# Attention with chunk selection, then a mixture over slots: a third ring buffer, a denser weight plan, and new orders of all steps

## The chip, the core and the metric

The kernel runs on one core of a Trainium2 chip. The metric is device time in microseconds (us) of one launch; lower is better. A core has engines that work side by side, each through its own list of instructions in order: PE (matrix products and transposes; its weight loads are shown as PEld), DVE (vector operations), ACT (activations and copies), POOL (here masks, small copies and the issue of loads) and SP (here the first two loads and the stores). Sixteen DMA engines carry the transfers. The kernel's tiles lie in on-chip memory; results of PE land in PSUM, eight banks of it.

## The reference, cut to what matters

B = 4, H = 8, S = 768, D = 64 for q, k, v; 8 experts with weights of 512 x 1024 and 1024 x 512; 32 slots, 4 for each expert.

```python
def _attn_ref(q, k, v):
    chunk, top_k, nc = 32, 6, S // 32
    k_min, k_max = per-chunk minimum and maximum of k
    ub = sum over d of max(q * k_min, q * k_max)        # bound of a chunk's scores
    ub = where(causal by chunk, ub, -1e9)
    top_chunks = argsort(ub)[..., -top_k:]
    scores = q @ k.T / sqrt(D)
    scores = where(chunk selected and causal, scores, -1e9)
    attn = softmax(scores)
    return attn @ v

def _moe_ref(x, phi, w1, w2):
    logits = x @ phi                                     # (3072, 32)
    d = softmax of logits over all 3072 rows
    slot_input = d.T @ x
    for e in range(8):
        slot_out[e] = relu(slot_input[e] @ w1[e]) @ w2[e]
    c = softmax of logits over the 32 slots
    return c @ slot_out
```

The rows x are the attention's outputs, so the last rows of the attention come before any slot is complete, and every output row needs all experts.

## The kernel before

**Pairs.** A pair is two heads of one batch: 16 pairs, four for each batch. For a pair, q and k are transposed on PE (`transposes`, L232) and evacuated by ACT (`evac_T`, L244). `kmin`, `kmax` and `heads` make the chunk bounds of k on DVE; `qneg` and `qpos` the two signs of q. `ubound` (L289) forms the bounds on PE, `select` (L312) takes the sixth largest on DVE with one small copy on POOL, `ns_transposes` and `evac_ns` turn the unselected chunks into a matrix that `scores` (L339) adds as a penalty. The scores come in six column groups (`GROUPS`; for the last pair `GROUPS_LAST`), each two heads wide in one of two PSUM tiles `p_sc`. `expo` (L363) exponentiates a group on ACT, `mask` (L376) clears the diagonal blocks on POOL, `pv` (L385) multiplies with v, `normalise` (L403) divides, `x_transposes` and `evac_x` give the transposed rows.

**Order.** The instructions of each engine stand in the order in which the program is written. A loop over pairs 1 to 15 reads one string of steps for each kind of pair: PLAIN, LOGITS, SLOTS, AFTER, BEFORE_LAST, FINAL. `sc:2` is the scores of group 2 of this pair, `ex`, `mk` its exponential and mask, `pv:0:1` products for query tiles 0 and 1 of the pair before, `trk`, `trq`, `evk`, `evq`, `kmin`, `kmax`, `bd`, `qsn`, `qsp` belong to the pair two ahead, `ub`, `sel`, `ns`, `evns` to the next pair, `norm`, `xt`, `evx` to the pair two behind. `evqd` is `evq` on DVE. Steps like `moe_logits@2` belong to the batch that ended two pairs ago: logits, maximum, exponentials, dispatch.

**Loads.** POOL issues all loads but the first two, in place in the order: `lv` v of a pair, `lkq` k and q of two pairs into a ring of two buffers (`load`, L160), `lw` as many weight blocks of 1 MB as `wplan` (L574) gives for the pair, `lh:n` a quarter of the last two experts' second weights (`w_half`, 256 KB; in the order of `HALVES`: both experts' upper output columns, then both lower). Weights 0 to 7 are w1; 8 to 13 are w2 of six experts. The first q and k arrive in f32 in the space of weight 13 and are cast (`cast`, L583).

**The end.** After pair 15 the last batch's slot softmax runs (L802 to L841), then the experts: `experts_in` (L870), `relu`, `hidden_T`, `experts_out(f)` for four experts over all 512 output columns, `shared_out(y, f)` and `last_expert_out(y)` for the other four over one half y of the columns. `so_all` holds the slots' outputs. For the first six blocks of 256 rows `out_half` writes the columns of half 1 and later those of half 0; the other six blocks are written whole. SP issues every store.

## Time and profile before

| what | us |
|---|---|
| median of 3 runs | 158.33 (158.31 to 158.43) |
| the profiled execution | 158.78 |
| its span, first to last instruction | 157.1 |
| PE, DVE, ACT, POOL busy | 137.4, 121.6, 121.2, 97.8 |
| bytes read and written | 52.49 MB, 6.29 MB |

Times in the rows below count from the span's start. A timeline row gives the start, the time taken, the engine, line, operation, output and inputs, how many such instructions follow one another, and in brackets how long the engine stood idle before and what ended that. A row of stretches gives the stretch, its length, each engine's busy time with the number of its instructions, the granted clock, the DMA engines' busy share and GB/s as written at the destination. A row of a DMA issue gives the number of transfers, their size and the time from issue to landing. In the slices of the span a digit is tenths of busy time.

### The profile page before, as it was taken

What the parts mean: (1) busy time and instruction counts of PE and PEld (TensorE: products, weight loads), DVE (VectorE), ACT (ScalarE), POOL (GpSimd) and SP (SyncE); (2) the same over time, 40 slices, a digit from 0 to 9 for tenths busy, and PEclk for the clock granted to TensorE, in tenths of its full rate; (3) what the DMA queues carried; (4) which work ended last, traced back from release to release, by engine and by line L of the source; (5) the groups of instructions that cost most, each with busy time, mean ns of one, the idle gap of its engine ahead of it and who ended that gap; (6) DMA issues with size and microseconds to landing.
All of it is one profiled execution on the core that took longest, in us unless ns stands there. A gap on an engine that the chain in (4) does not pass through costs nothing.

```text
span 157.1 us, 6041 instructions
## 1 busy us (share of the span) xinstructions
PE 137.4 (87%) x2485; PEld 91.1 (58%) x2486; DVE 121.6 (77%) x442; ACT 121.2 (77%) x172; POOL 97.8 (62%) x196
## 2 busy tenths in 40 slices
...
DMA  5999999999999999999999999999999999949995
GB/s 152 188 187 211 178 210 213 164 192 215 197 209 196 209 194 211 204 220 172 195 173 211 206 214 177 215 195 214 208 206 212 208 194 197 131 169 384 400 422 230
DMA packets 46171, 33.31 MB, mean 212 GB/s; under 512 B 26304, under 2 KB 41664, under 8 KB 46144
## 3 DMA queue, kind: packets, MB, share of 16 engines
q0 software_dynamic: 41328, 25.86, 113.5%
q1 hardware_dynamic: 4816, 7.08, 12.2%
...
HBM read 52.49 MB, written 6.29 MB: 374 GB/s over the span
## 4 chain that ended last, share of the span: by engine, by line
PE 58%; DVE 22%; ACT 7%; issue 3%; POOL 3%; DMA 2%; DVEq 0%; POOLq 0%; ACTq 0%
PE at_ps L398 11%; PE sc_ps L346 11%; PE sc_ps L356 8%; PE tr_ps L238 6%; ACT e_sb L370 4%; PE xT_ps L420 3%; PE ub_ps L296 3%; DVE mx L317 3%; DVE x_sb L411 3%; ACT o_sb L967 3%; PE h_ps L873 2%; DVE mm L256 2%; DVE mm L262 2%; DMA w_sb<-in_k_dram 2%; PE ns_ps L328 2%
## 5 line engine op out<-in xcount | busy, mean ns | idle before, releaser
L370 ACT ACTIVATE e_sb<-sc_ps 128x768 bf16<-128x768 f32 (+1 forms) x96 | 83.1, 926 | 6.5 <-PE sc_ps L356 5.1
L380 POOL TENSOR_SCALAR_AFFINE_SELECT e_sb<-e_sb 128x256 bf16<-128x256 bf16 x96 | 37.9, 417 | 22.0 <-ACT e_sb L370 21.8
L346 PE MATMUL sc_ps<-qT,kT 64*128 64x384 bf16 (+3 forms) x258 | 37.5, 308 | 2.3 <-ACT e_sb L370 2.0
L356 PE MATMUL sc_ps<-nsT,smask 64*128 64x384 bf16 (+2 forms) x294 | 37.7, 284 | 0.3
L398 PE MATMUL at_ps<-v_t,e_sb 128*128 128x65 bf16 x642 | 27.1, 194 | 0.4 <-DVE x_sb L411 0.2
L398 PEld LDWEIGHTS <-e_sb 128*128 128x128 bf16 x642 | 22.8, 97 | 6.5 <-POOL e_sb L380 2.9
L317 DVE MAX8 mx<-ub_ps 128x8 f32<-128x8 f32 (+1 forms) x192 | 16.9, 164 | 5.8 <-PE ub_ps L306 4.9
L346 PEld LDWEIGHTS <-kT 64*128 64x128 bf16 x258 | 12.6, 93 | 9.5 <-issue 3.5
L356 PEld LDWEIGHTS <-smask 64*128 64x128 bf16 x294 | 14.7, 95 | 3.8 <-issue 1.3
...
L411 DVE TENSOR_TENSOR x_sb<-at_ps,inv 128x768 bf16<-128x768 f32 (+1 forms) x17 | 15.5, 910 | 0.6
L247 ACT COPY kT<-tr_ps 128x768 bf16<-128x768 bf16 x16 | 12.8, 802 | 3.5 <-PE tr_ps L238 3.5
L256 DVE TENSOR_REDUCE mm<-kT 128x24 bf16<-128x768 bf16 x16 | 15.1, 944 | 0.4 <-ACT kT L247 0.4
L262 DVE TENSOR_REDUCE mm<-kT 128x24 bf16<-128x768 bf16 x16 | 15.1, 943 | 0.0
L247 ACT COPY qT<-tr_ps 128x768 bf16<-128x768 bf16 x14 | 11.5, 823 | 3.3 <-PE tr_ps L238 3.3
L145 POOL DMA_DIRECT2D w_sb<-in_moe_w_dram x14 | 10.2, 729 | 0.0
L296 PEld LDWEIGHTS <-qpn 128*128 128x128 bf16 x192 | 6.0, 96 | 6.7 <-issue 3.3
L431 DVE COPY xT_sb<-xT_ps 128x768 bf16<-128x768 bf16 (+1 forms) x15 | 8.0, 536 | 2.2 <-PE xT_ps L420 2.0
L296 PE MATMUL ub_ps<-bd,qpn 128*128 128x48 bf16 x192 | 7.8, 184 | 1.6 <-POOL qpn L276 1.4
L238 PE MATMUL tr_ps<-ident,k_in 128*64 128x128 bf16 x192 | 8.4, 223 | 0.7 <-DVE k_in L585 0.5
L420 PE MATMUL xT_ps<-ident,x_sb 128*128 128x128 bf16 x96 | 8.2, 220 | 0.3 <-DVE x_sb L411 0.3
L238 PE MATMUL tr_ps<-ident,q_in 128*64 128x128 bf16 x192 | 8.4, 223 | 0.0
(155 smaller groups left out, 216.3 us busy)
## 6 DMA issues: line engine op xcount, KB each, us to landing
w_sb<-in_moe_w_dram POOLq DMA_DIRECT2D x14, 1024.0 KB, 12.7
out_dram<-o_sb SPq DMA_DIRECT2D x14, 256.0 KB, 2.5
...
w_half<-in_moe_w_dram POOLq DMA_DIRECT2D x8, 256.0 KB, 11.5
...
```

The source lines that it names most:

```text
L238: nc.tensor.matmul(ps[h * 64:(h + 1) * 64, g, :], lhsT=src[:, h, g * D:(g + 1) * D], rhs=ident, is_transpose=True,)
L247: copy(t.rearrange("d (p g) -> d p g", g=NQT), st.pop((nm + "ps", i)).rearrange("d g p -> d p g"),)
L256: nc.vector.tensor_reduce(mm[:, 0, 0, :], kT, axis=AX.X, op=ALU.min)
L262: nc.vector.tensor_reduce(mm[:, 1, 0, :], kT, axis=AX.X, op=ALU.max)
L296: nc.tensor.matmul(o, lhsT=qpn[:, x, t * P:(t + 1) * P], rhs=bd[:, x], start=(t == 0 and x == 0), stop=False,)
L317: nc.vector.max(mx[:, a, :], ub[:, a, :max(8, 4 * t + 4)])
L346: nc.tensor.matmul(ps[:, h, c:c + w], lhsT=kT[r, kg * P:(kg + 1) * P], rhs=qT[r, qs], start=True, stop=False,)
L356: nc.tensor.matmul(ps[:, h, c + (f - t0) * P:c + (l - t0) * P], lhsT=smask[r, x, kg].rearrange("p a b -> p (a b)"), rhs=nsT[r, (f - x * NJ ...
L370: nc.scalar.activation(e[:, :, :w], st.pop(("scps", i, g))[:, :, :w], func=ACT.Exp, scale=scale)
L380: nc.gpsimd.affine_select(out=e[:, :, c:c + P], in_=e[:, :, c:c + P], compare_op=ALU.is_ge, fill=0.0, base=0, pattern=[[0, 2], [1, P]], ch ...
L398: nc.tensor.matmul(o, lhsT=st["e", i, g][:, h, c:c + P], rhs=v_t[i % NV][:, h, kg, :D + 1], start=(kg == 0), stop=(kg == t),)
L411: nc.vector.tensor_tensor(st["x", b][:, t0:t1, 2 * j:2 * j + 2, :].rearrange("p t h d -> p h t d"), at[:, :, :, :D], inv.broadcast_to([P, ...
```

## The change

- k and q get a third ring buffer, in the space of weight 10. `lkq` loads for pairs i + 7 instead of i + 5. `wplan` gives the same twelve blocks in fewer pairs.
- The first k and q lie in two weights' space and are cast by DVE (one head) and ACT (the other); k's transposes go to two PSUM tiles that ACT and DVE evacuate side by side. `qneg` of pair 0 goes from POOL to DVE. The warm-up products have 512 columns, in new numbers and places. Some first loads are issued earlier.
- Every order string is new. `evqd` is gone. FINAL now holds the last pair's own products, normalisations, transposes and logits in parts (`final`).
- The last pair's groups are cut anew: the sixth holds three off-diagonal blocks, all of query tile 5.
- The slot logits' maximum goes through PE as two bf16 parts instead of f32, and the same for the broadcast; the maximum over the first five tiles of the last batch is taken early (`pma`).
- The three exponentials of `exp_c` become one with windows of 24; `live`, which marks the columns that count, is made from `once` after pair 4.
- `experts_out` works on half of the columns like its neighbours; `so_part` is gone.

```diff
-    [(2, 0, 384, 0)],
-    [(4, 0, 256, 0), (2, 384, 128, 256)],
-    [(3, 0, 384, 0), (1, 512, 128, 384)],
-    [(5, 0, 128, 0), (0, 512, 256, 128)],
+    [(4, 0, 256, 0)],
+    [(2, 0, 384, 0), (0, 512, 128, 384)],
+    [(3, 0, 384, 0), (5, 0, 128, 384)],
+    [(0, 640, 128, 0), (1, 512, 128, 128), (2, 384, 128, 256)],
...
+    for x, nm in enumerate(("k", "q")):
+        spare = w_sb[EARLY - 4][:, x * 4 * NQT * D:(x + 1) * 4 * NQT * D]
+        ring[nm].append(spare.rearrange("p (h c) -> p h c", h=4))
...
-        t = ring[nm][i // 2 % 2][:, 2 * (i % 2):2 * (i % 2 + n)]
+        t = ring[nm][i // 2 % 3][:, 2 * (i % 2):2 * (i % 2 + n)]
...
-    stage = w_sb[EARLY - 1].bitcast(F32).rearrange("p (n h c) -> p n h c", n=2, c=512)[:, :, :, :NQT * D]
-    for n, (nm, src) in enumerate((("k", k), ("q", q))):
-        nc.sync.dma_start(out=stage[:, n], in_=src[0, :2].rearrange("h (p g) d -> p h (g d)", p=P))
+    stage = [w_sb[x].bitcast(F32).rearrange("p (h c) -> p h c", c=512)[:, :2, :NQT * D] for x in range(EARLY - 2, EARLY)]
+    for t, src in zip(stage, (k, q)):
+        nc.sync.dma_start(out=t, in_=src[0, :2].rearrange("h (p g) d -> p h (g d)", p=P))
+    load(1, "k")
...
+    def transposes(i, nm, runs=((0, NQT),), home=(p_tp, "tp")):
+
         src = st.pop((nm, i))
-        for g in range(NQT):
-            for h in range(2):
-                nc.tensor.matmul(
-                    ps[h * 64:(h + 1) * 64, g, :], lhsT=src[:, h, g * D:(g + 1) * D], rhs=ident,
-                    is_transpose=True,
-                )
-        st[nm + "ps", i] = ps
-
-    def evac_T(i, nm, copy=nc.scalar.copy):
+        st[nm + "ps", i] = []
+        for g0, g1 in runs:
+            ps = home[0].tile([P, g1 - g0, P], BF16, name="tr_ps", tag=home[1])
+            for g in range(g0, g1):
+                for h in range(2):
+                    nc.tensor.matmul(
+                        ps[h * 64:(h + 1) * 64, g - g0, :], lhsT=src[:, h, g * D:(g + 1) * D], rhs=ident,
+                        is_transpose=True,
+                    )
+            st[nm + "ps", i].append((g0, g1, ps))
...
+    def evac_T(i, nm, *copies):
 
         t = tp3.tile([P, S], BF16, name=nm + "T", tag=nm + "T")
-        copy(
-            t.rearrange("d (p g) -> d p g", g=NQT),
-            st.pop((nm + "ps", i)).rearrange("d g p -> d p g"),
-        )
+        for (g0, g1, ps), copy in zip(st.pop((nm + "ps", i)), copies or (nc.scalar.copy,)):
+            copy(
+                t.rearrange("d (p g) -> d p g", g=NQT)[:, :, g0:g1],
+                ps.rearrange("d g p -> d p g"),
+            )
...
+    def moe_logits(b, hgs=range(NDG), ps=None, ts=range(NQT)):
         phi = phi_sb
         if ps is None:
             ps = st["lgps", b] = p_tp.tile([P, NQT, NS], F32, name="lg_ps", tag="tp")
         else:
             phi = phi_sb.rearrange("p g (o s) -> p g o s", o=1).broadcast_to([P, NDG, 2, NS])
         xT = st["xT", b]
-        for t in range(NQT):
+        for t in ts:
             for hg in hgs:
                 nc.tensor.matmul(
                     ps[:, t, :], lhsT=xT[:, hg, t * P:(t + 1) * P], rhs=phi[:, hg],
-                    start=(hg == 0 and t == 0), stop=(hg == NDG - 1 and t == NQT - 1),
+                    start=(hg == 0 and t == 0),
+                    stop=(hg == NDG - 1 and t == (NQT - 2 if b == B - 1 else NQT - 1)),
+                    skip_group_check=(b == B - 1 and hg == NDG - 1 and t == NQT - 1),
                 )
+
+    def high(t):
+        return t.bitcast(BF16).rearrange("p (s x) -> p s x", x=2)[:, :, 1]
 
     def moe_copy(b):
         lg = small.tile([P, NQT, NS], F32, name="lg", tag="lg")
...
         nc.vector.tensor_copy(lg, ps)
         st["lg", b] = lg
 
+    def moe_lo(b, eng=nc.vector):
+        eng.tensor_tensor(pm_lo[:, :NS], pm_pad[:, :NS], high(pm_pad)[:, :NS], op=ALU.subtract)
+
     def moe_max(b):
 
         pmT = p_tp.tile([P, P], F32, name="pmT_ps", tag="tp")
-        nc.tensor.matmul(pmT, lhsT=pm_pad, rhs=identf, is_transpose=True)
+        nc.tensor.matmul(pmT, lhsT=high(pm_pad), rhs=ident, start=True, stop=False)
+        nc.tensor.matmul(pmT, lhsT=pm_lo, rhs=ident, start=False, stop=True)
...
+        mb_lo = small.tile([P, 1], BF16, name="mb_lo", tag="mb_lo")
+        nc.vector.tensor_tensor(mb_lo, mb, high(mb), op=ALU.subtract)
+        st["mb", b] = high(mb), mb_lo
...
-        nc.scalar.activation(c_pad[:, :, :, :SPE], c4[:, :, :4], func=ACT.Exp)
-        pairs = c4[:, :, 4:8]
-        pairs = bass.AP(pairs.tensor, pairs.offset, [list(x) for x in pairs.ap[:-1]] + [[1, 2 * SPE]])
-        nc.scalar.activation(c_pad[:, :, :, SPE:3 * SPE], pairs, func=ACT.Exp)
-        nc.scalar.activation(
-            c_pad[:, :, :, 3 * SPE:4 * SPE], c4[:, :, 4:5].broadcast_to([P, NQT, 4, SPE]), func=ACT.Exp)
+        c4 = lc[:, :NQT].rearrange("p t (j s) -> p t j s", s=SPE)[:, :, :4]
+        runs = bass.AP(c4.tensor, c4.offset, [list(x) for x in c4.ap[:-1]] + [[1, WIN]])
+        nc.scalar.activation(c_pad[:, :, :, :WIN], runs, func=ACT.Exp)
...
-    wplan = {2: 1, 3: 1, 4: 1, 5: 1, 6: 1, 9: 1, 10: 1, 11: 1, 12: 2, 13: 2, 14: 1, 15: 1}
+    wplan = {2: 2, 4: 1, 6: 2, 8: 1, 9: 1, 10: 1, 12: 2, 13: 2}
...
+    def cast(n, nm):
+        st[nm, 0] = ring[nm][0][:, :2]
+        nc.vector.tensor_copy(st[nm, 0][:, 0], stage[n][:, 0])
+        nc.scalar.copy(st[nm, 0][:, 1], stage[n][:, 1])
+
+    cast(0, "k")
     warm(8)
-    transposes(0, "k")
-    evac_T(0, "k")
+    transposes(0, "k", ((0, 3), (3, NQT)), (p_sc, "sc"))
+    cast(1, "q")
+    warm(1)
+    evac_T(0, "k", nc.scalar.copy, nc.vector.tensor_copy)
+    transposes(0, "q")
     kmin(0)
     kmax(0)
+    evac_T(0, "q")
+    load(4, "k", 2)
+    load_w(0)
     heads(0)
-    warm(2)
-    transposes(0, "q")
-    evac_T(0, "q")
-    qneg(0, nc.gpsimd)
-    load_w(0)
+    qneg(0)
...
+    warm(10)
     ubound(0)
-    transposes(1, "q")
-    evac_T(1, "q")
     spread_mask(NJ, NQT, nc.scalar.copy)
     select(0)
+    transposes(1, "k", ((0, NQT),), (p_sc, "sc"))
+    evac_T(1, "k")
+    transposes(1, "q", ((0, NQT),), (p_sc, "sc"))
+    evac_T(1, "q")
     load_v(1)
-    warm(5)
+    load(4, "q", 2)
+    warm(3)
     ns_transposes(0)
     evac_ns(0)
     kmin(1)
...
     heads(1)
     qneg(1)
     qpos(1)
+    for g in range(5):
+        scores(0, g)
+        expo(0, g, g < 4)
+        if g == 1:
+            load(6, "k", 2)
+            warm(3)
+        if g == 2:
...
-            if have(i + 5) and i % 2:
-                load(i + 5, "k", 2)
-                load(i + 5, "q", 2)
+            if have(i + 7) and i % 2:
+                load(i + 7, "k", 2)
+                load(i + 7, "q", 2)
...
-    PLAIN = """sc:0 trk sc:1 norm ub ex:0 ex:1 sc:2 lv mk:0 mk:1 evk pv:0 pv:5 sel sc:5 ex:2 xt trq lw pv:1:2:3 ex:5 evq sc:3 kmin sc:4 kmax ex:3 evx ns qsn mk:5 evns ex:4 mk:4 bd mk:2 lkq mk:3 pv:4 qsp"""
-    LOGITS = """sc:0 trk sc:2 ex:0 ex:2 ub norm sc:3 evk lv mk:0 ex:3 pv:0 pv:5 mk:2 pv:1 sc:1 sel xt trq pv:2:3 ex:1 evq sc:5 ex:5 mk:1 kmin sc:4 evx ns moe_logits@2 lw kmax bd evns mk:3 qsn ex:4 mk:5 mk:4 pv:4 lkq moe_copy@2 qsp"""
-    SLOTS = """sc:0 ex:0 moe_max@3 mk:0 sc:1 ex:1 mk:1 ub moe_bound@3 norm sel trk moe_comb@3 evk sc:2 pv:0 pv:1:2 lkq ex:2 sc:3 moe_exp@3 ex:3 mk:3 trq xt pv:3 kmin mk:2 evqd moe_exp2@3 evx kmax bd moe_scale@3 lw sc:4 ex:4 lv mk:4 sc:5 moe_comb2@3 ex:5 mk:5 ns pv:5:4 evns moe_dispatch@3 qsn qsp"""
-    AFTER = """sc:0 trk sc:1 ex:0 ex:1 evk mk:0 ub norm lv sc:2 ex:2 pv:0 sel pv:5 pv:1 sc:5 mk:1 xt pv:2:3 trq ex:5 sc:3 evq ex:3 kmin sc:4 evx ns mk:5 lw kmax pv:4 bdp evns mk:2 mk:3 ex:4 lkq mk:4 qsp moe_ct@4 qsn"""
-    BEFORE_LAST = """sc:0 ex:0 moe_max@3 sc:4 ex:4 mk:4 ub norm moe_bound@3 sel moe_comb@3 trk evk sc:2 mk:0 ex:2 pv:0 pv:1 pv:2:3 sc:1 ex:1 trq evq moe_exp@3 mk:2 mk:1 xt kmin kmax bd sc:3 lv evx lw ex:3 moe_exp2@3 moe_scale@3 pv:4 moe_comb2@3 sc:5 ex:5 mk:3 lkq mk:5 ns evns moe_dispatch@3 pv:5 qsp moe_ct3@3 qsn lh:0 lh:1"""
-    FINAL = """sc:0 ex:0 mk:0 lh:2 sc:1 ex:1 mk:1 lh:3 sc:2 norm ctc ex:2 pv:0:1:2 mk:2 sc:3 ex:3 xt mk:3 evx sc:4 ex:4 mz mk:4 pv:4:5:3 sc:5 ex:5 mk:5"""
+    PLAIN = """sc:0 trk lv sc:1 norm ex:0 ex:1 ub sc:2 pv:0 mk:0 evk pv:5 sel sc:5 mk:1 lw trq xt ex:2 pv:2 ex:5 evq pv:3:1 sc:3 kmin sc:4 kmax ex:3 ex:4 evx qsn ns mk:5 pv:4 mk:4 evns mk:2 mk:3 qsp lkq bd"""
+    LOGITS = """sc:0 trk sc:2 ex:0 ub norm ex:2 sc:3 evk mk:0 lv pv:0 pv:5 pv:1 mk:2 sc:1 sel ex:3 xt kmin pv:2 trq pv:3 ex:1 evq sc:5 lw ex:5 mk:1 sc:4 evx ns kmax bd mk:3 moe_logits@2 evns mk:5 qsn lkq ex:4 moe_copy@2 moe_lo@2 mk:4 qsp pv:4"""
+    SLOTS = """sc:1 ex:1 mk:1 moe_max@3 sc:2 ex:2 mk:2 ub moe_bound@3 norm sel moe_comb@3 trk evk sc:0 sc:3 ex:0 moe_exp@3 lkq ex:3 mk:3 pv:0:1:2:3 trq xt kmin evq moe_exp2@3 evx kmax bd moe_scale@3 lv lw sc:5 ex:5 mk:5 sc:4 ex:4 mk:4 ns evns mk:0 moe_dispatch@3 pv:5 moe_comb2@3 qsn qsp pv:4"""
+    AFTER = """sc:0 lv trk sc:2 ex:0 ex:2 evk ub sc:1 norm pv:0 pv:5 sel ex:1 pv:2 pv:3 mk:0 sc:3 pv:1 mk:2 xt trq lw ex:3 sc:5 kmin evx evq ex:5 sc:4 ns mk:1 kmax bdp pv:4 mk:5 evns ex:4 mk:4 lkq qsp moe_ct@4 mk:3 qsn"""
+    BEFORE_LAST = """lv norm sc:2 ex:2 moe_max@3 sc:4 ex:4 sc:0 moe_bound@3 moe_comb@3 mk:4 lw ub sel sc:3 pv:0 trk evk pv:2 moe_exp@3 pv:3:4:5:1 mk:2 ex:0 trq evq kmin sc:5 ex:3 mk:0 moe_comb2@3 kmax moe_exp2@3 xt ns sc:1 moe_scale@3 mk:3 lkq qsn ex:5 lh:0 evx mk:5 ex:1 qsp lh:1 evns moe_dispatch@3 moe_ct3@3 bd mk:1"""
+    FINAL = """sc:1 sc:0 norm sc:2 ex:1 pv:0 pv:2 pv:3 pv:4 mk:1 ctc pv:5 pv:1 ex:0 ex:2 sc:3 xt mk:0 ex:3 norm1 sc:4 mk:2 ex:4 xt1 mk:3 evx pl:0 evx1 sc:5 mk:4 pl:2 pl:1 nl:0 pl:3 nl:1 xl:0 pl:4 lgt el:0 mz lh:2 ex:5 pl:5 lh:3 xl:1 cs nl:2 lgl:0 xl:2 ela:1 lgl:1 ela:2 pma lgl:2 inv"""
...
+    PARTS = [
+        (0, [(0, 0), (1, 0), (2, 0), (1, 1), (2, 1), (2, 2)], True, True),
+        (1, [(3, 0), (3, 1), (4, 1), (4, 4), (3, 2), (4, 2), (4, 0)], True, False),
+        (2, [(5, 4)], True, False),
+        (1, [(3, 3), (4, 3)], False, True),
+        (2, [(5, 3), (5, 5)], False, False),
+        (2, [(5, 0), (5, 1), (5, 2)], False, True),
+    ]
+    SPANS = [(0, 3), (3, 5), (5, 6)]
...
+        elif name == "pl":
+            pv_part(*PARTS[n])
+        elif name == "nl":
+            normalise(LAST, *SPANS[n], part(n)[0])
+        elif name == "xl":
+            x_transposes(LAST, *SPANS[n])
+        elif name in ("el", "ela"):
+            evac_x(LAST, *SPANS[n], nc.scalar.copy if name == "ela" else nc.vector.tensor_copy)
+        elif name == "lgt":
+            st["lgt"] = p_at.tile([P, 2, 512], F32, name="lgt_ps", tag="at")
+            st["lg12"] = st["lgt"][:, 0, :2 * NQT * NS].rearrange("p (t o s) -> p t o s", t=NQT, o=2)
+            moe_logits(BL, range(NDG - 1), st["lg12"])
+        elif name == "lgl":
+            moe_logits(BL, range(NDG - 1, NDG), st["lg12"], range(*SPANS[n]))
+        elif name == "pma":
+            nc.vector.tensor_reduce(
+                pm_a, st["lg12"][:, :NQT - 1, 0, :].rearrange("p t s -> p s t"), axis=AX.X, op=ALU.max)
...
-    nc.vector.tensor_reduce(pm, lg1.rearrange("p t s -> p s t"), axis=AX.X, op=ALU.max)
+    nc.vector.tensor_tensor(pm, pm_a, lg1[:, NQT - 1], op=ALU.max)
...
+    mneg_lo = small.tile([NS, 1], BF16, name="mneg_lo", tag="mneg_lo")
+    nc.vector.tensor_tensor(mneg_lo, mneg, high(mneg), op=ALU.subtract)
     bc = p_tp.tile([P, NS], F32, name="bc_ps", tag="tp")
-    nc.tensor.matmul(
-        bc, lhsT=mneg.broadcast_to([NS, P]), rhs=identf[:NS, :NS], start=True, stop=True,
-    )
+    for n, part in enumerate((high(mneg), mneg_lo)):
+        nc.tensor.matmul(
+            lg2, lhsT=part.broadcast_to([NS, P]), rhs=rep.broadcast_to([NS, NQT, NS]),
+            start=False, stop=(n == 1), skip_group_check=True,
+        )
+        nc.tensor.matmul(
+            bc, lhsT=part.broadcast_to([NS, P]), rhs=ident[:NS, :NS], start=(n == 0), stop=(n == 1),
...
+    def experts_out(y, f):
         for fg in range(f * 4, (f + 1) * 4):
             for e in range(4):
+                w0 = fg * Dm + y * HD
                 nc.tensor.matmul(
-                    so_ps[e * CH:(e + 1) * CH, :], lhsT=hT_pad[:, fg, e, :],
-                    rhs=w_sb[E + e][:, fg * Dm:(fg + 1) * Dm], start=(fg == 0), stop=(fg == NFG - 1),
+                    outs[y][e * CH:(e + 1) * CH, :], lhsT=hT_pad[:, fg, e, :],
+                    rhs=w_sb[E + e][:, w0:w0 + HD], start=(fg == 0), stop=False,
...
-    experts_out(0)
+    experts_out(1, 0)
+    shared_out(1, 0)
     hidden_T(1)
-    shared_out(1, 0)
     slot_sums()
-    experts_out(1)
+    experts_out(1, 1)
     shared_out(1, 1)
     last_expert_out(1)
-    nc.scalar.activation(so_sb[1], so_ps[:, HD:], func=ACT.Copy, scale=zinv)
-    nc.scalar.activation(so_part, so_ps[:, :HD], func=ACT.Copy, scale=zinv)
+    nc.scalar.activation(so_sb[1], outs[1], func=ACT.Copy, scale=zinv)
     TAGS = (("tp", "tp"), ("sc", "at"))
     for m in range(BYHALF):
         out_half(m, 1, TAGS[m % 2])
-    shared_out(0, 0)
-    shared_out(0, 1)
+    for f in range(2):
+        experts_out(0, f)
+    for f in range(2):
+        shared_out(0, f)
     last_expert_out(0)
-    nc.vector.scalar_tensor_tensor(so_sb[0], so_last, zinv, so_part, op0=ALU.mult, op1=ALU.add)
+    nc.vector.tensor_scalar_mul(so_sb[0], outs[0], zinv)
```

225 lines of the change are left out of this document (107 added, 118 removed).

## The prediction

> **What bounds it.** I read the slices, the queues and the issue list first, then stretches of the loop and of the end, then the timeline around four places: the start, the last pair, the expert products, the stores.
>
> ```profile
> DMA  5999999999999999999999999999999999949995
> q0 software_dynamic: 41328, 25.86, 113.5%
> q1 hardware_dynamic: 4816, 7.08, 12.2%
> L380 POOL TENSOR_SCALAR_AFFINE_SELECT e_sb<-e_sb 128x256 bf16<-128x256 bf16 x96 | 37.9, 417 | 22.0 <-ACT e_sb L370 21.8
> ```
>
> The DMA engines are busy from the first slice to the last. Queue q0 carries the loads that POOL issues (25.86 MB as written, in bf16), q1 the first two loads and the stores. One transfer in the stream shows how full it is:
>
> ```profile
> 15.03 0.74 POOL L145 DMA_DIRECT2D w_sb<-in_moe_w_dram  x1
> w_sb<-in_moe_w_dram POOLq DMA_DIRECT2D x1, 1024.0 KB, 14.6
> ...
> 119.72 0.76 POOL L155 DMA_DIRECT2D w_half<-in_moe_w_dram  x1
> w_half<-in_moe_w_dram POOLq DMA_DIRECT2D x1, 256.0 KB, 13.4
> ...
> L155 POOL DMA_DIRECT2D w_half<-in_moe_w_dram x8: 740/748/821, 116.2 to 128.1; - x8
> w_half<-in_moe_w_dram POOLq DMA_DIRECT2D x1, 256.0 KB, 10.2
> ```
>
> A weight load of 1 MB issued at 15.03 lands 14.6 us later, a 256 KB one at 119.72 lands 13.4 later (133.1), the last one (issued at 128.1) 10.2 later (138.3 to 138.4). None is ever answered at once: POOL runs 10 us and more ahead, and the stream itself is the clock. Its end:
>
> ```profile
> 137.00:138.00 1.00, 0.60 (x4) 0.39 (x4) 0.29 (x1) 0.90 (x3) 0.00 (x0) 1.00 0.14 19
> ...
> 139.50:140.00 0.50, 0.50 (x15) 0.25 (x17) 0.50 (x2) 0.40 (x3) 0.00 (x0) 1.00 0.73 260
> 140.00:141.00 1.00, 0.81 (x32) 0.52 (x20) 0.45 (x2) 0.45 (x2) 0.00 (x0) 1.00 1.09 383
> ```
>
> The rate has fallen to 19 GB/s before the last load lands: most of the 16 engines are done by 137, the slowest at 138.4. Then next to nothing moves until the first store's data, about 139.6, and from 140 the stores run at 383 GB/s with the engines full (share 1.09). So the span is a load stream, a gap, and a store stream. What joins them is this:
>
> ```profile
> 133.16 1.04 PE L912 MATMUL so_ps<-w_sb,hT_pad 128*32 128x512 bf16 x16
> 136.88 0.47 ACT L992 ACTIVATE so_all<-so_ps,zinv 128x256 bf16<-128x256 f32 x1 [2.89 <-PE so_ps L947]
> 138.36 0.62 SPq L983 DMA_DIRECT2D out_dram<-o_sb  x1
> 140.93 0.48 DVE L1000 SCALAR_TENSOR_TENSOR so_all<-so_last,zinv,so_part 128x256 bf16<-128x256 f32 x1 [0.55 <-ACT o_sb L967]
> 142.45 3.96 SPq L983 DMA_DIRECT2D out_dram<-o_sb  x6
> ```
>
> The first half of the columns leaves at 138.36, the second half at 142.45. From 142.45 on, the other six half stores, five full ones and two quarter ones follow at the engines' rate to the end: 157.1 − 142.45 = 14.65 us. The end is therefore **the start of the second store group plus 14.65**, and two rails lead to that start: the compute, and the last weight load, which the second half's last products need. I call the first store T1 and that start S2.
>
> **The start** (`cast`, `transposes`, `evac_T`, `qneg`, `warm`).
>
> ```profile
> 1.47 0.86 POOL L163 DMA_DIRECT2D k_in<-in_k_dram  x1
> 4.17 0.80 DVE L585 CAST k_in<-w_sb 128x768 bf16<-128x768 f32 x1 [0.97 <-DMA w_sb<-in_k_dram]
> 5.15 0.83 DVE L585 CAST q_in<-w_sb 128x768 bf16<-128x768 f32 x1 [0.18 <-DMA w_sb<-in_q_dram]
> 6.42 0.95 DVE L256 TENSOR_REDUCE mm<-kT 128x24 bf16<-128x768 bf16 x1 [0.44 <-ACT kT L247]
> 7.50 2.14 POOL L276 TENSOR_SCALAR qpn<-qT 128x768 bf16<-128x768 bf16 x1 [0.60 <-ACT qT L247]
> 9.69 0.47 PE L296 MATMUL ub_ps<-bd,qpn 128*128 128x48 bf16 x12 [1.40 <-POOL qpn L276]
> 13.15 4.37 ACT L370 ACTIVATE e_sb<-sc_ps 128x1024 bf16<-128x1024 f32 x5 [0.92 <-PE sc_ps L356]
> ```
>
> The k cast (0.80) and the evacuation of k are split over two engines, but ACT now casts its half of q, which lands at 5.12, before it evacuates k: cast to about 5.6, copy to 6.1 (half of 0.80 plus issue). kmin then starts near 6.15 instead of 6.42, 0.3 us sooner. Two reductions and the head product take until 8.2. The 2.14 us of POOL for qneg becomes a DVE instruction behind them (0.35 to 0.57 in later pairs), so ub_ps can start near 8.6 to 8.8, against 9.69. Ten warm-up matmuls of 512 columns (about 2.1 us) lie in that wait of PE. Everything behind, up to the first exponential at 13.15, keeps its order of dependence. Gain 0.3 (if the earlier POOL load slows the q load) to 1.1; I take 0.8. POOL's first load no longer stands behind the identity's select: 1.47 becomes about 0.9, and the stream may end up to 0.6 sooner; I take 0.3. Dropping the memsets of `live` frees DVE time that ends in its wait for k: nothing, and nothing if the cover goes but 0.4.
>
> **The load stream** (third buffer, `wplan`, `load` at i + 7). The same bytes cross the same 16 engines, which have no idle slice to fill; loads issued sooner only wait longer. So the stream's end stays at 138.37 − 0.3 = 138.1, and the third buffer itself is worth nothing. Its price is on POOL: in the compiled order each load waits for the landing of the eighth before it. Weight 1, which landed at 29.6, gets k and q of pairs 6 and 7 ahead of it (2 x 384 KB at 200 GB/s, 3.9 us) and lands near 33.5; v of pair 5 is to be issued at the start of pair 3, which stood at 19.35 + 2 x 26.00/4 = 32.35 (the loop's first row below) and now at 31.55, and waits for it. POOL stands 1.95 us, with pair 3's masks and the POOL part of pair 4's selection behind it; the latter is needed some 5 us into the pair, and POOL idles 22 us over the kernel waiting for ACT (the select row above). I take 0; if the cover fails in all of pairs 2 to 4, a loss near 3.
>
> **The loop** (PLAIN to AFTER, `evqd` gone, bf16 halves for the f32 matmuls, one exponential).
>
> ```profile
> 19.35:45.35 26.00, 25.70 (x490) 17.00 (x486) 23.32 (x89) 25.50 (x33) 17.85 (x36) 1.00 1.41 200
> 45.35:73.34 27.99, 27.85 (x554) 19.19 (x552) 26.74 (x98) 25.97 (x36) 19.98 (x41) 1.00 1.31 203
> 73.34:102.19 28.85, 28.04 (x553) 19.26 (x552) 27.07 (x98) 26.30 (x37) 21.25 (x44) 1.00 1.44 197
> 116.50:123.00 6.50, 5.82 (x121) 4.30 (x120) 3.62 (x9) 5.18 (x6) 5.48 (x10) 1.00 1.06 214
> ...
> L516 ACT ACTIVATE c_pad<-lc_sb x4: 270/274/284, 59.0 to 128.4; 128x96 bf16<-128x96 f32 x4
> L519 ACT ACTIVATE c_pad<-lc_sb x4: 347/352/354, 59.2 to 128.6; 128x192 bf16<-128x192 f32 x4
> ```
>
> Pairs 1 to 4 (first row) hold ACT 25.50 of 26.00: eight ACT instructions a pair that no edit touches, so no reordering helps there. The next two groups of four pairs have ACT 25.97 of 27.99 and 26.30 of 28.85, DVE 26.74 and 27.07. The new order gives ACT back one q evacuation a group (0.82) and takes 0.95 from DVE, adding two short subtractions. Three slot exponentials (96, 192 and 96 elements) become one of 576: 96 more elements cost 0.08 by the last two rows, so 0.35 + 4 x 0.08 = 0.67 for a sum of 0.9, 0.2 at most, nothing in view of their overlap. ACT's floor, 26.8 and 27.1, bounds the gain at 1.2 + 1.7 = 2.9; the lane wait above bounds the loss at 3. PE is shown as busy for nearly the whole of every group, so I take 0.
>
> **The last pair** (GROUPS_LAST, FINAL, `pma`, bf16 maximum).
>
> ```profile
> 122.19 0.81 ACT L370 ACTIVATE e_sb<-sc_ps 128x768 bf16<-128x768 f32 x1 [0.49 <-POOL siT_pad L731]
> 124.17 0.56 DVE L411 TENSOR_TENSOR x_sb<-at_ps,inv 128x384 bf16<-128x384 f32 x1
> 125.88 0.36 DVE L804 TENSOR_REDUCE pm<-lgt_ps 128x32 f32<-128x192 f32 x1 [0.36 <-PE lgt_ps L443]
> 126.95 0.59 PE L820 MATMUL lgt_ps<-identf,mneg 32*128 32x192 f32 x2
> 127.64 0.33 ACT L829 ACTIVATE d_sb<-lgt_ps 128x192 bf16<-128x192 f32 x1 [2.60 <-PE lgt_ps L820]
> ```
>
> The last of the pair's six exponentials ends at 123.0; ACT is busy 5.18 of the 6.50 us to there (the row of 116.50 above), of which the first 0.65 is the lead of its first scores. With the products of the pair before spread between the scores, 0.5 of the other 0.67 goes. Behind the last exponential the old chain is mask, 14 products, a reduction over three tiles (0.56), transposes, copy, 24 logit products, maximum to 126.24: 3.24 (its select, products and transposes stand between the rows shown). The last group now has no diagonal block (no mask) and one query tile: six products 0.3, reciprocal 0.19, one third of the 0.56 plus fixed part 0.3, transpose 0.22, copy 0.27, logit 0.2, maximum 0.19, seven hops of 0.06: 2.1, gain 1.15. The f32 broadcast (0.59) becomes two bf16 passes with one subtraction between: gain 0.2. Together 1.85; bounds 0.5 (the DVE list of four normalisations and three copies in a row, about 4 us, ends last) and 2.2.
>
> **The expert products.** `experts_out(1, ...)` has 256 columns for 512: half of the 1.04 shown for 16 products at 133.16, twice, is 1.0; 0.75 after the pipeline's lead of some 0.1 each. So compute puts T1 at 138.36 − 0.8 − 1.85 − 0.75 = 134.95. The load rail allows the same: the fourth w_half lands at 133.1 − 0.3; half of `last_expert_out`, so_all (0.47) and the 1.0 us from so_all to the first store make 134.6. I take **T1 = 134.9**. `so_part` (0.47 of ACT) goes, in the shadow of DVE's copies. Between the halves PE now has the 32 products moved there (0.9) and shared_out and last_expert_out as before: compute allows S2 at T1 + 4.9 = 139.8.
>
> **What the early stores cost.** Data of a store flows 1.3 us after issue (138.36 to about 139.6): from 136.2. The slowest engines still have 138.07 − 136.2 = 1.9 us of loads. Before, the two streams never met there. Bounds: the loads do not notice (138.1), or all six half stores go first (six of 256 KB at 383 GB/s, 0.68 each, 4.1: 142.2). The packets cost much the same by the queue rows (16 engines x 157.1 us: 1.135 / 41328 gives 69 ns, 0.122 / 4816 gives 64), so I take turns packet for packet, 1.9 x (1 + 64/69) = 3.7: **139.9**. [...] No stretch of this trace has both queues full, so it is untested.
>
> **The sum.** From the last landing: half of last_expert_out 0.2, so_all 0.48 with hops 0.1, and 1.04 from its end (141.41) to 142.45: 1.8. S2 = 139.9 + 1.8 = 141.7, later than compute's 139.8. Gain 142.45 − 141.7 = 0.75, span 156.35. This execution took 158.78 with its span of 157.1, so 158.0 for one like it; the median of the runs shown is 158.33, so I predict 157.6.
>
> **Rivals.** (1) The loads do not notice the stores: S2 = 139.9, by both rails, gain 2.5, 155.8. For it: most engines are idle by 137; against: the last landing is that of the slowest, on which stores lie too. (2) The stores go first: landing 142.2, S2 144.0, **1.55 later: 159.9**. Its place is those slowest engines between 136 and 140; it turns slower once the landing passes 140.65, that is, when stores take over 57% of them. Nothing in the trace excludes it. (3) The compute rail falls back: POOL's lane waits cost the 3 us above. Then T1 = 137.9, the streams do not meet, S2 = 142.8 from compute: 158.6; a loss under 2.3 there still leaves a gain, one of 1 would even be the best case (T1 135.9, loads at 138.9, S2 140.8, 156.7), since stores and loads then miss each other. (4) The change does to the stream what it says, with bytes earlier: against it, no idle slice before the gap.
>
> **How the numbers follow.** Forecast 0.5 (its own range 156.6 to 158.0: T1 from 134.6 to 136.9), rival 1 0.2, rival 2 0.1, rival 3 0.18, rival 4 0.02. Range 155.4 to 159.3: down to rival 1 with the stream's full 0.6 at the start, up over rival 3 and into rival 2. A change under 0.2%, 0.3 us, can't be told from none. Faster: forecast, rivals 1 and 4 and the milder third of 3 without the edges of the forecast, 0.7; same 0.12; slower 0.18.
>
> **What would show it.** First exponential near 12.35; POOL's v of pair 5 waiting for a landing near 33; pairs 1 to 4 at 6.5 each; first store near 135, while q0 still moves bytes; last w_half landing between 139 and 141, later than 138.4; second group of stores 1.8 behind it. I am wrong if the last landing stays at 138 with stores under way, if S2 follows T1 by 4.9 (compute decides), or if the load stream ends before 137.

## The result, and the profile after

The changed kernel takes **157.88 us** (median of 16 runs, 156.85 to 161.34), the kernel before 158.77 on the same chip (16 runs, 158.30 to 160.23): ratio 0.993, 95% interval 0.9902 to 0.9957. The profiled execution took 157.53 with a span of 155.8, before 158.78 and 157.1. In five of the 16 runs PE's granted clock, as a mean over the span, is 0.967 to 0.969 and the span 156.2 to 159.6; in the other eleven, the profiled one among them, it is 0.977 to 0.987 and the span 155.1 to 156.3.

Where the 1.3 us of span come from, point by point along the chain (times from the two profiled executions):

| point | before | after | earlier by |
|---|---|---|---|
| first exponential | 13.15 | 12.44 | 0.71 |
| first scores of pair 5 | 45.35 | 45.18 | 0.17 |
| first scores of pair 9 | 73.34 | 72.75 | 0.59 |
| first scores of pair 13 | 102.19 | 100.37 | 1.82 |
| first scores of the last pair | 116.50 | 114.70 | 1.80 |
| maximum of the last logits done | 126.24 | 124.63 | 1.61 |
| so_all of the first half | 136.88 | 134.18 | 2.70 |
| first store, T1 | 138.36 | 135.67 | 2.69 |
| second group of stores, S2 | 142.45 | 140.55 | 1.90 |
| end | 157.1 | 155.8 | 1.3 |

The start, in the timeline (start, time taken, engine, line, operation; in brackets the idle time before it and what ended that):

```profile
4.70 1.06 POOL L174 DMA_DIRECT2D v_t<-in_v_dram  x1
5.13 0.81 DVE L591 CAST q_in<-w_sb 128x384 bf16<-128x384 f32 x1 [0.85 <-DMA w_sb<-in_q_dram]
...
6.55 0.95 DVE L259 TENSOR_REDUCE mm<-kT 128x24 bf16<-128x768 bf16 x1
...
8.57 0.35 DVE L279 TENSOR_SCALAR qpn<-qT 128x768 bf16<-128x768 bf16 x1
...
8.99 0.47 PE L299 MATMUL ub_ps<-bd,qpn 128*128 128x48 bf16 x12 [0.20 <-DVE qpn L279]
...
12.44 4.37 ACT L373 ACTIVATE e_sb<-sc_ps 128x1024 bf16<-128x1024 f32 x5 [0.94 <-PE sc_ps L359]
```

The split casts and copies bring nothing: the minimum of k starts at 6.55, before at 6.42. The rows show why: DVE's cast of its half of q starts inside POOL's issue of v and takes 0.81 us, where its half of k took 0.36, and DVE's copy of k stands behind it. In e4_fills_later and e8_old_experts, where q landed 0.2 us sooner, the same cast took 0.36 and the minimum began at 6.25 and 6.01. The 0.70 at ub_ps (9.69 to 8.99) is `qneg` alone, 0.35 on DVE for 2.14 on POOL.

The loop in the stretches that were shown of before, and the last pair to its last exponential (length; busy time and count of PE, PEld, DVE, ACT, POOL; clock; DMA share; GB/s):

```profile
18.64:45.18 26.54, 25.43 (x491) 17.23 (x488) 24.18 (x92) 25.61 (x33) 20.20 (x43) 1.00 1.44 198
45.18:72.75 27.57, 27.24 (x551) 19.18 (x551) 26.29 (x99) 26.68 (x35) 20.52 (x42) 1.00 1.39 201
72.75:100.37 27.62, 27.29 (x553) 19.23 (x552) 26.58 (x99) 26.80 (x36) 18.90 (x41) 1.00 1.36 200
114.70:121.93 7.23, 6.55 (x142) 5.11 (x141) 5.15 (x13) 5.37 (x7) 4.35 (x10) 1.00 1.15 215
```

Pairs 1 to 4 take 26.54 for 26.00 and give most of the start's gain back. The next two groups take 0.42 and 1.23 less; the second of them, 27.62 with ACT busy 26.80, is close to the floor of 27.1 that the prediction named. The last pair takes 7.23 to its last exponential, before 6.50.

The end, in the timeline:

```profile
134.18 0.47 ACT L1056 ACTIVATE so_all<-so_ps,zinv 128x256 bf16<-128x256 f32 x1 [1.97 <-PE so_ps L1011]
...
135.67 8.81 SPq L1047 DMA_DIRECT2D out_dram<-o_sb  x12
...
138.63 0.39 PE L1011 MATMUL so_last<-w_half,hT_pad 128*32 128x256 bf16 x8
139.08 0.48 DVE L1065 TENSOR_SCALAR so_all<-so_last,zinv 128x256 bf16<-128x256 f32 x1 [1.37 <-PE so_last L1011]
...
140.55 3.93 SPq L1047 DMA_DIRECT2D out_dram<-o_sb  x6
```

The last weight half and the first store as single DMAs (KB, us from issue to landing), the stores in stretches, and the store queue's row of the page (packets, MB, share of 16 engines):

```profile
w_half<-in_moe_w_dram POOLq DMA_DIRECT2D x1, 256.0 KB, 10.1
...
out_dram<-o_sb SPq DMA_DIRECT2D x1, 256.0 KB, 3.2
```

```profile
138.00:142.00 4.00, 2.95 (x53) 2.00 (x42) 2.48 (x6) 1.84 (x5) 0.00 (x0) 1.00 1.04 347
142.00:146.00 4.00, 2.94 (x23) 1.32 (x21) 3.17 (x7) 2.62 (x6) 0.00 (x0) 1.00 1.04 345
...
q1 hardware_dynamic: 4816, 7.08, 12.8%
```

And the kernel before, from its S2 on:

```profile
142.40:146.00 3.60, 2.32 (x20) 1.32 (x20) 3.21 (x7) 2.59 (x6) 0.00 (x0) 1.00 1.09 383
```

Issued at 128.10, the last half lands at 138.2, no later than before (138.4), though store data has flowed since 137. PE's last products start at 138.63 without a wait: S2 follows T1 by 4.88, so the compute decides it. And behind S2 the end takes 15.25, not 14.65: with the DMA engines full the stores move 345 to 347 GB/s for 383, and the same 4816 packets take 12.8% x 16 x 155.8 / 4816 = 66 ns each for 64. In neither kernel do the engines run empty at S2: the share is 1.04 on both sides of it, before 1.09. The second group's data follow the first group's without a gap, so in these two kernels an S2 that came sooner, with T1 as it is, would only have found a longer queue.

### The profile page after: what moved, and what is told of

The parts are those of the page before. It is cut to its first block, busy times and chain, and to the rows that moved or that the text cites. A ratio compares the mean times of both kernels' runs of the same rounds, so it can differ in the third digit from the quotient of the medians.

```text
span 155.8 us, 6087 instructions
## 1 busy us (share of the span) xinstructions
PE 138.0 (89%) x2515; PEld 90.9 (58%) x2515; DVE 122.4 (79%) x450; ACT 122.4 (79%) x167; POOL 95.3 (61%) x196
## 3 DMA queue, kind: packets, MB, share of 16 engines
q1 hardware_dynamic: 4816, 7.08, 12.8%
## 4 chain that ended last, share of the span: by engine, by line
PE 47%; DVE 23%; ACT 12%; issue 5%; POOL 4%; DMA 2%; DVEq 0%; SPq 0%; ACTq 0%; POOLq 0%
PE sc_ps L349 9%; PE at_ps L397 9%; ACT e_sb L373 8%; PE sc_ps L359 6%; PE tr_ps L240 4%; PE xT_ps L419 3%; DVE mx L320 3%; DMA w_sb<-in_q_dram 2%; PE h_ps L934 2%; DVE mm L259 2%; DVE mm L265 2%; PE ub_ps L299 2%; ACT o_sb L1031 2%; POOL e_sb L383 2%; DVE o_sb L1034 2%
## 5 line engine op out<-in xcount | busy, mean ns | idle before, releaser
L373 ACT ACTIVATE e_sb<-sc_ps 128x768 bf16<-128x768 f32 (+2 forms) x96 | 83.1, 927 | 5.5 <-PE sc_ps L359 4.6
L397 PE MATMUL at_ps<-v_t,e_sb 128*128 128x65 bf16 x630 | 26.3, 193 | 0.2
L410 DVE TENSOR_TENSOR x_sb<-at_ps,inv 128x768 bf16<-128x768 f32 (+3 forms) x18 | 15.6, 868 | 0.6
L250 ACT COPY qT<-tr_ps 128x768 bf16<-128x768 bf16 x16 | 13.1, 816 | 1.4 <-PE tr_ps L240 1.4
L250 ACT COPY kT<-tr_ps 128x768 bf16<-128x768 bf16 (+1 forms) x16 | 12.7, 796 | 0.1
L230 PE MATMUL warm_ps<-ones_sq 128*128 128x512 bf16 x29 | 9.2, 451 | 1.1 <-DVE ones_sq L180 1.1
L430 DVE COPY xT_sb<-xT_ps 128x768 bf16<-128x768 bf16 (+1 forms) x16 | 8.6, 536 | 1.2 <-PE xT_ps L419 1.2
L323 DVE TENSOR_TENSOR ns_t<-ub_ps,mx 128x288 bf16<-128x288 f32 x16 | 7.3, 457 | 0.5
```

The lines of the kernel that those rows point to most:

```text
L250: copy(t.rearrange("d (p g) -> d p g", g=NQT)[:, :, g0:g1], ps.rearrange("d g p -> d p g"),)
L373: nc.scalar.activation(e[:, :, :w], st.pop(("scps", i, g))[:, :, :w], func=ACT.Exp, scale=scale)
L397: nc.tensor.matmul(o, lhsT=st["e", i, g][:, h, c:c + P], rhs=v_t[i % NV][:, h, kg, :D + 1], start=(kg == 0), stop=(kg == t),)
L410: nc.vector.tensor_tensor(st["x", b][:, t0:t1, 2 * j:2 * j + 2, :].rearrange("p t h d -> p h t d"), at[:, :, :, :D], inv.broadcast_to([P, ...
```

## The experiments

Each kernel is the changed kernel with the edit shown, if nothing else is said. Times are medians; the ratio is to the kernel before, measured together with them (158.75 for e1 to e4, 158.94 for e5 to e8 and e12, 159.33 for e9 to e11). Times of different groups are best compared by their ratios.

| run | us (runs) | ratio, 95% interval |
|---|---|---|
| changed kernel | 157.88 (16) | 0.993 (0.9902 to 0.9957) |
| e1_old_slots | 162.81 (4) | 1.0251 (1.0166 to 1.0336) |
| e2_two_buffers | 157.22 (9) | 0.9925 (0.9893 to 0.9957) |
| e3_scores_first | 157.89 (10) | 0.9971 (0.9939 to 1.0004) |
| e4_fills_later | 157.94 (10) | 0.9941 (0.991 to 0.9972) |
| e5_aligned | 156.80 (6) | 0.9871 (0.9831 to 0.9911) |
| e6_old_slots_v_first | 159.55 (10) | 1.0033 (1.0005 to 1.0061) |
| e7_early_stores | 159.95 (1), with 1 MB more stores | none |
| e8_old_experts | 158.40 (10) | 0.9965 (0.993 to 1.0001) |
| e9_early_norm | 156.84 (4) | 0.9836 (0.978 to 0.9891) |
| e10_seven | 157.05 (6) | 0.9851 (0.9804 to 0.9899) |
| e11_before_off | 160.22 (10) | 1.0074 (1.0039 to 1.011) |
| e12_pool_later | 156.55 (6) | 0.9845 (0.9794 to 0.9896) |

### Why the stores are slow: the address of the output tiles

```diff
+    pad_32 = tail.tile([P, 8], F32, name="pad_32")
```

> The changed kernel with one unused tile of 32 bytes a partition ahead of the output tiles, and nothing else. In the changed kernel, without so_part and with new small tiles, the output tiles begin 32 bytes off a multiple of 64 (137440 = 64 x 2147 + 32), in the kernel before on one (137984 = 64 x 2156); its half stores land 0.76 us apart for 0.70, and the stores move 344 to 349 GB/s at a DMA share of 1.04 for 383 to 385 at 1.09. Theory: the store packets are slower for their address in SBUF. Then the half stores of the second group land 0.70 apart again, the stores move 383 GB/s, and the time from the second group's start to the end is 14.6 to 14.7 for 15.25: span 0.6 under the changed kernel's, 155.2 if the rest runs as in its profile. Rival: the slower stores come from their meeting the loads, or differ from run to run: 0.76 apart and 15.25 again.

The theory holds. The store stretch and the queue's row:

```profile
143.00:145.00 2.00, 1.08 (x10) 0.66 (x12) 1.34 (x4) 0.62 (x2) 0.00 (x0) 1.00 1.09 384
...
140.37 3.91 SPq L1048 DMA_DIRECT2D out_dram<-o_sb  x6
...
q1 hardware_dynamic: 4816, 7.08, 12.3%
```

From 140.37 to the end at 155.0 it takes 14.6, and the span falls by 0.8. The counterpart puts the same tile into the kernel before:

> The kernel before with one unused tile of 32 bytes a partition ahead of the output tiles, which puts them 32 bytes off a multiple of 64 (138016). Theory: this alone costs what the changed kernel lost behind the second group's start. Half stores of the second group 0.76 apart for 0.70, time from there to the end 15.2 for 14.65, span 157.6 to 157.7, time up by 0.6. Rival: the address matters only beside the changed kernel's earlier stores: 14.65 and no change.

```profile
140.00:143.00 3.00, 2.10 (x40) 1.45 (x40) 2.07 (x6) 1.55 (x4) 0.00 (x0) 1.00 1.01 344
143.00:146.00 3.00, 1.91 (x14) 1.00 (x12) 2.76 (x6) 2.28 (x6) 0.00 (x0) 1.00 1.01 343
...
142.75 4.34 SPq L984 DMA_DIRECT2D out_dram<-o_sb  x6
```

344 GB/s for 383, and 15.75 behind S2 (span 158.5): 1.1 us, not 0.6. Here the second group comes while the first is still in the queue (its first store takes 3.0 us to land, for 2.5 in the kernel before), so the first group's loss counts too. The start address alone does it, with or without loads beside it. All good cases were also multiples of 256 (137984, 137472), so the runs don't say whether 64 or 256 is the boundary.

### What earned the loop's gain: the order of SLOTS

```diff
-    SLOTS = """sc:1 ex:1 mk:1 moe_max@3 ... pv:0:1:2:3 trq xt kmin evq moe_exp2@3 ... lv lw sc:5 ...
+    SLOTS = """sc:0 ex:0 moe_max@3 mk:0 ... ex:3 mk:3 trq xt pv:3 kmin mk:2 evqd moe_exp2@3 ... lw sc:4 ex:4 lv ...
```

> The changed kernel with the old order of steps in the SLOTS pairs (6 and 10) and nothing else put back. In the changed kernel the lead over the kernel before grows by 0.42 us in pair 6 and by 0.82 in pair 10, and stands at 1.80 at the first exponential of the last pair (115.35). Theory: the order of the SLOTS steps earns this. Then pairs 6 and 10 take 0.4 and 0.8 longer again, the last pair's first exponential comes near 116.6, the first store near 136.9 and the second group of stores near 141.8, span 157.0. Rival: the one exponential in place of three and the bf16 maximum, which stay in, earn it: first exponential of the last pair by 115.8, span within 0.4 of 155.8.

Far off both: the greater part of the loss, 3.8 us, lies in pair 9, where PE waits 2.26 us for a v and ACT then 2.69 us for scores. The old order issues v behind the weights, and the new `wplan` gives pair 6 two of them:

```profile
58.35 1.46 POOL L150 DMA_DIRECT2D w_sb<-in_moe_w_dram  x2
59.80 1.04 POOL L174 DMA_DIRECT2D v_t<-in_v_dram  x1
...
78.46 0.89 PE L397 MATMUL at_ps<-v_t,e_sb 128*128 128x65 bf16 x18 [2.26 <-DMA v_t<-in_v_dram]
...
80.36 1.02 ACT L373 ACTIVATE e_sb<-sc_ps 128x1024 bf16<-128x1024 f32 x1 [2.69 <-PE sc_ps L359]
```

That v lands 18.5 us after its issue, at 78.3; in the changed kernel, a place ahead of the weights, at 68.6. With `lv` put ahead of `lw`:

> The changed kernel with the old order of the SLOTS steps (pairs 6 and 10), but with the load of v issued ahead of the weights as in the new order: in the first try the v of pair 8 stood behind the two weights of pair 6 in the queue, landed at 78.33 for 68.61 and held up pair 9. Theory: the order of SLOTS earns the loop's gain. Then pairs 6 and 10 take 0.4 and 0.8 us longer than in the changed kernel, its lead of 1.80 at the last pair falls to 0.4 to 0.8, first store 136.7 to 137.1, second group 141.6 to 142.0, span 156.9 to 157.2. Rival: the one exponential and the bf16 maximum earn it: lead 1.4 or more, first store by 136.1.

From the first exponential to the last pair's first one it takes 104.39 (13.62 to 118.01; in this execution q landed late) for 102.91 in the changed kernel, 1.48 longer; pairs 6 and 10 alone are 8.02 each for 7.48 and 7.53, and the pairs behind them 7.13 and 7.14 for 6.72 and 6.71. The theory holds. The old order's ACT in pair 10, then the new one's:

```profile
87.27 0.36 ACT L502 ACTIVATE d_sb<-ld 128x192 bf16<-128x192 f32 x1 [0.72 <-POOL ld L490]
```

```profile
84.32 0.80 ACT L250 COPY qT<-tr_ps 128x768 bf16<-128x768 bf16 x1
85.13 0.36 ACT L502 ACTIVATE d_sb<-ld 128x192 bf16<-128x192 f32 x1
...
87.12 0.68 ACT L527 ACTIVATE c_pad<-lc_sb 128x576 bf16<-128x576 f32 x1
```

The old order leaves ACT idle for 0.72 until POOL has made `ld`, while DVE does the q evacuation; the new one has ACT do it in just that wait. By the ratios the old order costs 1.0% (1.0033 for 0.993). The end of the profiled execution is not compared: PE's clock fell in it behind 129, as the last section tells.

### The third buffer and the weight plan

```diff
-        t = ring[nm][i // 2 % 3][:, 2 * (i % 2):2 * (i % 2 + n)]
+        t = ring[nm][i // 2 % 2][:, 2 * (i % 2):2 * (i % 2 + n)]
...
-    wplan = {2: 2, 4: 1, 6: 2, 8: 1, 9: 1, 10: 1, 12: 2, 13: 2}
+    wplan = {2: 1, 3: 1, 4: 1, 5: 1, 6: 1, 9: 1, 10: 1, 11: 1, 12: 2, 13: 2, 14: 1, 15: 1}
```

> The changed kernel with two ring buffers for k and q, loads five pairs ahead and the old plan of the weights. Theory: the load stream is full from the first slice, so when a load is issued does not matter: last weight half lands at 138.2 (within 0.3), first store 135.7 and second group 140.55 (within 0.3), span 155.8 within 0.4. The POOL wait for a landing at v of pair 5 (35.00 in the changed kernel) goes. Rival: the third buffer carries part of the loop's gain, as a k or q load that POOL has to hold back until a buffer is free holds back its masks: then the last pair starts 0.5 or more later than 115.35 and the span is 156.4 or more.

Span 155.7, the ratio inside the changed kernel's interval: worth nothing, as predicted. T1 is 135.40, the last half lands at 138.64 and S2 stands at 140.49, 5.1 behind T1 but 1.85 behind that landing: here the load rail decides, at the 1.8 that the prediction had worked out for it.

### Where the start's gain went: pair 1

```diff
+        if i == 3:
+            nc.gpsimd.dma_start(out=phi_sb, in_=moe_phi.rearrange("(hg p) s -> p hg s", p=P))
+            nc.vector.memset(pm_pad, 0.0)
+            nc.vector.memset(pm_lo, 0.0)
+            nc.gpsimd.affine_select(
...
```

> The changed kernel with POOL's phi load and its fills of identf and once, and DVE's fills of pm_pad and pm_lo, moved from pair 1 to the start of pair 3. In the changed kernel the lead of 0.71 us falls to 0.11 in pair 1, where DVE's qneg takes 0.63 for 0.35 while POOL works beside it and PE waits 0.68 for it. Theory: POOL's fills slow DVE there. Then qneg takes 0.35 again, pair 2's first exponential comes at 25.9 to 26.1 (26.51 in the changed kernel), and the lead is kept: last pair's first exponential at 114.8 to 115.0, first store 135.1 to 135.3, second group not before 140.0, span 155.3 to 155.5. Rival: the fills only move the loss to pair 3, or a later pair eats the lead: last pair's first exponential within 0.2 of 115.35, span 155.8.

Missed: pair 2's first exponential stays at 26.55, and pairs 3 and 4 lose 0.5 more. POOL's and DVE's rows of this kernel in pair 1:

```profile
20.12 1.08 POOL L174 DMA_DIRECT2D v_t<-in_v_dram  x1
...
20.49 0.87 DVE L289 TENSOR_SCALAR qpn<-qT 128x768 bf16<-128x768 bf16 x1
```

With the fills gone the v load came forward and stood beside `qpos` (0.87) in place of `qneg`. So the fills were the wrong suspect; what both cases share is a load issue of POOL beside `qneg` or `qpos`. A second try, on e5_aligned, keeps every load issue out of 20.2 to 21.0 (the fills stand behind the second masks of pairs 1 and 2):

```diff
+        if i == 1:
+            order = order.replace(" lv ", " ", 1).replace(" mk:0 ", " mk:0 lv ", 1)
```

> e5_aligned with POOL's v of pair 3 behind the first mask of pair 1, its fills of identf and once behind the second one, and the phi load and DVE's fills of pm_pad and pm_lo in pair 2. In the changed kernel, in e4_fills_later and in e5_aligned the lead of 0.6 to 0.7 us falls to 0.0 to 0.1 in pair 1; in each a POOL load issue stood beside DVE's qneg or qpos, and the one beside it took 0.63 or 0.87 for 0.35 (in e4_fills_later the fills were gone and the v load hit qpos in their place). Theory: it is the load issue beside these two that costs the lead. With none beside them (20.2 to 21.0) both take 0.35, pair 2's first exponential comes at 25.9 to 26.2 for 26.5 to 26.6, and the lead at the last pair is 0.3 to 0.5 larger (114.7 to 114.9). The end gains 0.2 at most, since the second group stands 1.8 behind the last landing: span 154.7 to 155.0. Rival: something else holds pair 1: pair 2 at 26.4 or later.

```profile
20.22 0.35 DVE L279 TENSOR_SCALAR qpn<-qT 128x768 bf16<-128x768 bf16 x1
20.49 0.35 DVE L289 TENSOR_SCALAR qpn<-qT 128x768 bf16<-128x768 bf16 x1
...
21.05 1.02 POOL L174 DMA_DIRECT2D v_t<-in_v_dram  x1
```

Both take 0.35, and pair 2's first exponential comes at 26.03. Pairs 3 and 4 give 0.4 of it back; the last pair's stands at 114.98, 0.2 ahead of e5_aligned. Span 154.6, and with 156.55 the shortest median of the study, shorter than both kernels; its interval overlaps with those of e5_aligned, e9_early_norm and e10_seven, so the runs don't rank these four. That the load issue costs the lead in pair 1 is shown; what that is worth at the end is within the noise.

### The last pair

```diff
-... pv:0 pv:2 pv:3 pv:4 mk:1 ctc pv:5 pv:1 ex:0 ex:2 sc:3 xt mk:0 ex:3 ...
+... pv:0 pv:2 pv:3 mk:1 ctc ex:0 ex:2 sc:3 pv:4 pv:5 pv:1 xt mk:0 ex:3 ...
```

> The changed kernel with the scores of group 3 of the last pair moved ahead of 26 of the 42 products that stand before them. In the changed kernel ACT waits 1.07 us for these scores at 118.85 and the last exponential ends at 121.93. Theory: the block of products starves ACT. Then this wait shrinks to 0.4 or less, the last exponential ends near 121.2, the maximum of the logits (124.44) comes 0.4 to 0.7 sooner, the first store at 135.0 to 135.3, and the second group follows by 4.9 but not before 140.0 (last landing 138.2 and 1.8): span 155.3 to 155.5. Rival: DVE's list of normalisations and copies ends last in this pair: the exponential ends sooner but the maximum stays within 0.2 of 124.44, first store 135.6, span 155.8. If stores took turns with loads, the earlier stores would push the last landing past 138.5.

First the changed kernel, with a row of stretches at its end, then this one:

```profile
116.43 0.28 PE L349 MATMUL sc_ps<-qT,kT 64*128 64x256 bf16 x2 [0.68 <-ACT e_sb L373]
...
116.75 1.45 PE L397 MATMUL at_ps<-v_t,e_sb 128*128 128x65 bf16 x42
...
118.24 0.23 DVE L409 RECIPROCAL inv<-at_ps 128x12 f32<-128x12 f32 x1 [1.29 <-PE at_ps L397]
...
118.85 2.00 ACT L373 ACTIVATE e_sb<-sc_ps 128x1024 bf16<-128x1024 f32 x2 [1.07 <-PE sc_ps L359]
...
124.44 0.19 DVE L866 TENSOR_TENSOR pm<-pm_a,lgt_ps 128x32 f32<-128x32 f32 x1
...
116.43:123.80 7.37, 7.37 (x177) 6.15 (x176) 4.73 (x13) 4.55 (x7) 4.50 (x9) 1.00 1.07 212
```

```profile
118.07 1.02 ACT L373 ACTIVATE e_sb<-sc_ps 128x1024 bf16<-128x1024 f32 x1 [0.28 <-PE sc_ps L359]
...
118.91 0.23 DVE L409 RECIPROCAL inv<-at_ps 128x12 f32<-128x12 f32 x1 [1.98 <-PE at_ps L397]
...
120.19 0.51 PE L419 MATMUL xT_ps<-ident,x_sb 128*128 128x128 bf16 x6 [0.44 <-DVE x_sb L410]
...
121.66 0.81 ACT L373 ACTIVATE e_sb<-sc_ps 128x768 bf16<-128x768 f32 x1 [0.78 <-PE sc_ps L359]
```

The wait of 1.07 shrinks to 0.28 and that exponential comes 0.78 sooner, but the last one 0.54 later: the products now end later, with them the division (118.91 for 118.24) and the transposes, behind which the last scores stand in PE's list. The maximum comes at 124.98, 0.54 later. Neither the theory nor the rival came out. What the pair ends on is PE's list: from 116.43 to 123.80 its instructions make 7.37 of 7.37 us, while DVE (4.73) and ACT (4.55) wait for it again and again, and the chain that ended last runs through PE alone in this stretch. Where PE has no idle time, a wait of ACT that an order closes is paid for elsewhere; here PE even waits 0.44 more, for DVE's division, which is most of the 0.54. (Behind 126.5 PE's clock fell in this execution, so its T1 isn't used; the shortest of the ten spans is 155.8, the changed kernel's 155.1.) A second try, on e5_aligned, starts the products sooner; the division `norm` now stands in BEFORE_LAST:

```diff
-... sc:1 sc:0 norm sc:2 ex:1 pv:0 pv:2 pv:3 ...
+... sc:1 sc:0 ex:1 pv:0 pv:2 sc:2 pv:3 ...
```

> The changed kernel with the output tiles on a multiple of 64 bytes (as in e5_aligned), the division of pair 13 moved from the last pair into pair 14, where DVE is idle for 0.9 and 0.8 us near 112 to 114.5, the first products of the last pair ahead of its third scores, one filler matmul ahead of the last logits and two instead of one behind the last moe_dispatch. In the changed kernel the products of pair 14 start 1.40 us after the last pair's first exponential (116.75, 115.35), since their accumulator is read by that division until 116.49; the maximum of the logits comes 9.1 behind that exponential (124.44) and the first store 20.3 behind it. Theory: DVE's list, which starts with the products, ends last in this pair. Then the products start 0.5 behind the exponential, the maximum 8.2 to 8.5, the first store 19.4 to 19.7 behind it (134.6 to 135.0). The second group gains little of this: it stands 1.8 to 1.9 behind the last landing (138.46 in e5_aligned), 140.2 to 140.4, span 154.8 to 155.0. Rival: the list is not the end of it, the maximum stays 9.1 behind. Rival for the end: the second group follows the first by 4.9 whatever the loads do, span 154.4. No run should show a clock of 0.969 or less if the fillers keep it up.

```profile
116.80 0.28 PE L349 MATMUL sc_ps<-qT,kT 64*128 64x256 bf16 x2 [0.33 <-ACT e_sb L373]
```

The first products start 0.33 us behind the first exponential (116.05, 115.72), yet the maximum comes 8.85 and T1 20.09 behind it: 0.24 of the 0.7. Only eight products get ahead; the other 34 wait in PE's list behind the third scores, and those for the first exponential's PSUM tile. That wait, the one idle time of PE ahead of the last logits, shrinks from 0.68 to 0.33; behind it PE is busy without a gap again, so this edit could win no more than this 0.35. As to the end, the rival is right: the last half had landed at 137.1, S2 followed T1 by 4.87 (135.81, 140.68), span 155.1. Whether the fillers keep PE's clock up can't be told from four runs.

### What the halved expert products are worth

```diff
-    experts_out(1, 0)
+    experts_out(0)
...
-    for f in range(2):
-        experts_out(0, f)
```

> The changed kernel with the old end of the experts: expert products 512 columns wide ahead of the first stores, so_part by ACT, and only the shared products between the halves. Theory: the products only changed places. The first store comes 0.8 to 0.95 us later (136.5 for 135.67), the second group follows by 4.1 for 4.88 and starts within 0.15 of 140.55, the end within 0.3 of 155.8. Rival: the first group's head start is worth something to the store stream, since a queue that starts sooner has more of the bytes behind it when the second group comes: then the span grows by 0.5 to 0.9.

T1 136.27 and S2 140.33, 4.06 apart; this execution ran 0.31 us ahead at the last pair's first exponential, so on equal footing T1 is 0.91 later and S2 0.1: the products changed places. But the end is 156.1, 15.8 behind S2. The rival is right: with slow stores (the output tiles begin at 138464 here, again 32 bytes off a multiple of 64) the queue is still full when the second group comes, and on equal footing the head start is worth 0.6. By the ratios it is 0.35% (0.9965 for 0.993) with intervals that overlap, so the size rests on the two profiles.

### Stores that meet the loads

```diff
+    early = o_tiles[BYHALF - 1][:, :, HD:]
+    nc.gpsimd.memset(early, 0.0)
+    for m in range(8, 12):
+        nc.sync.dma_start(out=rows(m)[:, :, HD:], in_=early)
```

> The changed kernel with four more stores of 256 KB (zeros, to rows that are written again later) issued by SP after the first layer of the experts, near 131, while the load queue is full and every DMA engine has loads. Theory from the changed kernel's profile: loads hardly notice stores; then the last weight half lands by 138.6 (138.19 in the changed kernel) and each of the early stores takes 4 us or more for 2.5. By turns packet for packet, as the prediction had it, 1 MB of stores at 383 GB/s costs 2.7 us of the engines while it runs beside the loads: the last half lands at 140 to 141. Stores first: the same 2.7, and the early stores land in 2.5 each. Rival of a bound elsewhere: the loads are held by their reads from HBM and not by the engines, then both go at full speed, the stores land in 2.5 to 3 and the loads at 138.2 to 138.4.

The four stores went out from 132.20. The queues between 134 and 135 (packets, MB, share of 16 engines), first in the changed kernel, then with the early stores:

```profile
q0 software_dynamic: 229, 0.11, 83.5%
```

```profile
q0 software_dynamic: 223, 0.11, 81.9%
q1 hardware_dynamic: 172, 0.17, 47.4%
...
out_dram<-o_sb SPq DMA_DIRECT2D x2, 256.0 KB, 6.6
...
w_half<-in_moe_w_dram POOLq DMA_DIRECT2D x1, 256.0 KB, 11.0
```

No theory as put. In the four us from 133 on the loads keep their packets: 358, 223, 191 and 50 with the stores, 364, 229, 188 and 52 without. A full load queue shows a share of 1.44, so 82% is an estimate of nine engines; 47% of the stores' 1.09 is the other seven. So the stores seem to move on engines that have run out of loads, and a store that needs all of them takes 6.1 to 6.6 us. The rows don't say which engine a packet runs on, so this is argued and not shown. At the very end it is otherwise: seven of the eight halves keep their spacing of 1.3 to 1.4, but the last lands at 139.06, 2.7 behind the seventh, about twice the time, as turns would have it. In e5_aligned, without the extra stores, it comes 2.5 behind as well, in the changed kernel 1.4. Why stores hold up the last half in some executions and not in others stays open.

### More of the stores ahead of S2

```diff
-    BYHALF = 6
+    BYHALF = 7
...
     for m in range(BYHALF):
         out_half(m, 1, TAGS[m % 2])
+        if m in (2, 3):
+            experts_out(0, m - 2)
...
```

> e9_early_norm with seven blocks stored by halves instead of six, and the products of the second half of the columns put between the first half's blocks. Theory: the second group has to wait for the last landing in any case, so a seventh half store fits ahead of it; what is left behind the second group's start is 256 KB less, 0.68 us at 383 GB/s: time from there to the end 13.9 to 14.0 for 14.64, second group at 140.2 to 140.6, span 154.2 to 154.6. Rival: the seventh half pushes the second group back by its own 0.7 (ACT and DVE need 0.7 for each half block): second group at 141, span 155.0.

T1 is 135.16, the last half lands at 138.59, S2 comes at 140.54, and the end 14.9 later, at 155.4 (six runs, 154.3 to 155.4): no gain. The first half store of each group takes 4.1 and 3.5 us to land, so stores still queue up somewhere. Yet the engines as a whole run half empty ahead of the second group's data (share 0.55 between 140.4 and 141.2, for 1.09), while the stores go on landing 0.7 us apart without a gap. That fits one engine, the one that finishes its loads last, with a queue that never runs out: from the last load's landing to the last store's it is 15.8 us here, 15.5 in e5_aligned (138.46, 153.93) and 15.7 in e12_pool_later (137.78, 153.52). In e9_early_norm, whose loads ended at 137.1 and whose second group came late, it is 16.9. So it is a third rail, on which the first three kernels seem to lie; the rows don't show single engines.

## Why the prediction was right

The time came out 0.3 above the forecast, in its range and on its side. The 0.3 is the base: the sum was taken off 158.33, the median of three runs, where 16 runs give 158.77; the gain was 0.89 for the 0.75 forecast. The sum did not hold term by term, and that it came out so near is in part luck.

- **Start: right in sum** (0.8; 0.71), by `qneg` alone. The 0.3 of the split casts did not come, since DVE's cast of q met POOL's load issue. The load stream ends 0.2 sooner for 0.3.
- **The third buffer and the weight plan: right** (nothing). POOL stood 0.46 us ahead of the v of pair 5 (35.00) for the 1.95 worked out. In e1_old_slots the denser plan cost 3.8 us where v stood behind two weights; the prediction had asked what POOL waits for, and not what queues behind the weights.
- **The loop: mis-sized** (0; 1.09). PE "busy for nearly the whole of every group" was no limit: ACT's waits in two pairs were what the order could close, and the bound from ACT's floor was the better guide. The loss of 0.54 in pairs 1 to 4 was not in it: it sought POOL's cost in late masks, and in pair 1 it lay in DVE's `qneg` beside a load issue. The single exponential takes 0.68, as estimated (0.67).
- **The last pair: wrong in size** (1.85, bounds 0.5 to 2.2; about 0: 1.80 at its first scores, 1.61 at its maximum and 0.17 back at the broadcast). The step that failed adds up the chain behind the last exponential as if PE were free for it. That part did shrink, from 3.24 to 2.70, but the pair's products now stand ahead of the last exponential and push it from 6.50 to 7.23 behind the first scores. PE's list is what ends last: from the first exponential to the maximum it was busy for 7.89 of 9.09 us before and for 8.11 of 9.28 now. The lower bound named DVE's list, which in the trace waits for PE.
- **The expert products: right at T1** (0.75; 0.92). That 0.79 of it goes again between the halves was in the step "T1 + 4.9 = 139.8", which was exact at 4.88.
- **What the early stores cost: wrong for this kernel.** The last half landed at 138.2, not 139.9, in the spacing of the halves before it, and compute decided S2, as "I am wrong if" had it. Turns packet for packet were the author's estimate, and no run shows them as a rule: by them the loads would have lost time as soon as both queues were full; in e7_early_stores they lost none up to the seventh half, and only the last half took twice as long (2.7 us for 1.3 to 1.4). The 223 load packets for 229 between 134 and 135 don't look like turns, the last half does, and the rows, whose packets hold 0.5 and 1 KB (0.11 MB in 229, 0.17 in 172) and which show no single engine, can't decide it.
- **The sum: two errors that cancel.** S2 was 140.55 for 141.7, but "14.65" behind it, taken as fixed, became 15.25, since dropping `so_part` and adding small tiles moved the output tiles 32 bytes off a multiple of 64. Nor was "the start of the second store group plus 14.65" the rule it was taken for: the engines were full on both sides of S2, so the end hung on T1 and the whole store stream as much. With the address put right it is 156.8 (e5_aligned), 0.8 under the forecast and still inside the range.
